# Eleven row groups of w2 by column halves instead of thirteen, and another grouping of the output rows

## The chip, the cores and the metric

The kernel runs on one core of a Trainium2 chip. The metric is the device time of one execution in microseconds (us); lower is better. A core has a matrix engine (TensorE, "PE" in the profile, with its weight loads as "PEld"), a vector engine (VectorE, "DVE"), a scalar engine (ScalarE, "ACT"), GpSimd ("POOL") and SyncE ("SP"). In this kernel GpSimd hands over the loads and SyncE the stores. The data are moved by 16 DMA engines that all queues share. Matmul results land in PSUM, in eight banks of 128 partitions x 512 f32, and have to be evicted from there to SBUF by VectorE or ScalarE before they can be stored.

## What is computed

Attention with eightfold mean-pooled keys and values (8 batches, 8 heads, 576 positions, 64 per head) gives 4608 tokens x of width 512. A soft mixture of experts follows, with 8 experts of 4 slots each (32 slots). The change touches only what stands in the last lines, the second layer and the combine.

```
logits = x @ phi                               # 4608 x 32
d = softmax of logits over the tokens;  slot_input = d.T @ x
for e in range(8):
    h = max(slot_input[e] @ w1[e], 0)          # 4 x 1024
    slot_out[e] = h @ w2[e]                    # w2[e]: 1024 x 512
c = softmax of logits over the slots
out = c @ slot_out                             # 4608 x 512, f32
```

All weights come as f32 and are turned into bf16 by the loads.

## The kernel before, in words

Until about 112 us the kernel runs the attention in four pairs of batches. The weights w1 and w2 stream in behind the attention's inputs, all through GpSimd's one queue, in the order in which the code issues them.

**w2 and its pieces.** The 1024 rows of one expert's w2 lie in SBUF as 128 partitions x 8 row groups (`FJ` = 8) of 512 columns. Experts 0 to 3 go to `big` and 4 and 5 to `qTa`, whole. Expert 6 (`E - 2`) is cut: its first `CUT6` = 3 row groups come in full width (line 507). Its other five, and all eight of expert 7 (`E - 1`), come by column halves of 256 columns, `halves` (line 91): first all thirteen groups for the left half, then all thirteen for the right. `PIECES` (line 92) lists them: five groups of expert 6, then four, three and one of expert 7, one DMA each (lines 526 to 533). So the left half of `slot_out` is complete before the right half of the last weights has arrived, and the left half of the output can be stored meanwhile. `half_home` gives each piece its place in `xsa`.

**The second layer.** `second_layer` (line 576) adds row groups into the one PSUM tile `so_ps`. TensorE's order is written out by hand (lines 680 to 711). Between the pieces stand dummy matmuls, `busy(n)` (line 611), which write to a tile nobody reads, so that TensorE isn't idle.

**The tail.** `begin(half, stores)` (line 652) ends one column half. For the first four tiles of 128 tokens (`CARRY` = 4) the last row group isn't waited for twice: ScalarE copies what `so_ps` holds without it, scaled, to `so_a`, and four matmuls on `zT` (line 659) put the last group's share straight into the output banks; four more (line 662) add the rest from `so_a`. Then the last row group goes into `so_ps` (line 663), VectorE copies it to `so` (line 667), and from `so` come all other tiles (`product`, line 636). Each tile is evicted with the scale of its rows by `put(n, cols, engine, ps)`, where engine 0 is ScalarE (line 616) and 1 VectorE (line 618). `tiles(n0, n1, half)` does two tiles and stores them. Tiles 0 to 9 are done by halves, left then right; the other 26 in full width after that. Five PSUM banks turn over for these products.

**The grouping of the rows.** `GROUPS` (line 57) says how many rows of the output each partition holds in a group of tiles: 2, 2, 2, 4, 4, 8 and 14, 36 tiles in all. Tile r of a group of n rows holds the tokens base + n x p + r for partition p, so that a group of n rows is stored with n rows of 512 f32 in one run per partition. `tokens(n)` (line 456) picks the right columns of `cT`. `out_a` (the space of `exa`) holds the first six tiles on their way out, `out_b` (the space of `w1_sb`) the others (lines 623 to 630).

**The stores.** SyncE issues them in the order of the code: for the left half four stores of one tile each (in `begin`) and three of two tiles; for the right half five of two tiles; then a group of 4, one of 8 and one of 14 rows in full width, 1, 2 and 3.5 MB.

Of the kernel before, what the change touches and what calls it, by code (L numbers as in the profile page):

```python
# [18 lines left out]
def kernel(  # L19
# [10 lines left out]
    nc = tc.nc  # L30
# [5 lines left out]
    E = moe_w1.shape[0]  # L36
# [12 lines left out]
    FJ = F // 128  # L49
# [4 lines left out]


    GROUPS, base = [], 0
    for rows in (2, 2, 2, 4, 4, 8, 14):
        GROUPS.append((rows, base))
        base += 128 * rows
    TILES = [(g, r) for g, (rows, _) in enumerate(GROUPS) for r in range(rows)]  # L60
# [13 lines left out]
    cT = persist.tile([128, 2, B * S // 2], BF)  # L74
# [11 lines left out]

    CUT6 = FJ - 5
    HC = DM // 2  # L90
    halves = [slice(0, HC), slice(HC, DM)]
    PIECES = ((E - 2, CUT6, FJ), (E - 1, 0, 4), (E - 1, 4, FJ - 1), (E - 1, FJ - 1, FJ))

# [15 lines left out]
    def load_w2(home, e, n, j0=0, j1=FJ):  # L109
        for i in range(n):  # L110
            for j in range(j0, j1):
                w2_at[e + i, j] = home[:, i, j * DM:(j + 1) * DM]
        nc.gpsimd.dma_start(out=home[:, 0:n, j0 * DM:j1 * DM],
                            in_=moe_w2[e:e + n].rearrange("e (p j) d -> p e j d", j=FJ)[:, :, j0:j1].rearrange("p e j d -> p e (j d)"))
# [49 lines left out]
    with tc.tile_pool(name="tmp", bufs=1) as tmp:  # L164
# [8 lines left out]
        for r in range(2):  # L173
            rows = slice(r * D, (r + 1) * D)
# [11 lines left out]
        for r in range(2):  # L186
            rows = slice(r * D, (r + 1) * D)
# [219 lines left out]
    for g, (rows, base) in enumerate(GROUPS):  # L407
        cols = cT[:, :, base // 2:base // 2 + 64 * rows].rearrange("p r (i s) -> p s r i", s=rows // 2)
# [44 lines left out]
        nc.vector.reciprocal(out=recR[:, 2:4, 0:len(quads)], in_=ps[:, 2:4, 0:len(quads)])  # L453
        yield

    def tokens(n):

        g, r = TILES[n]
        rows, base = GROUPS[g]
        step, c0 = rows // 2, base // 2 + r // 2  # L460
        return cT[:, r % 2, c0:c0 + 127 * step + 1:step]

    def step(gen):
        if gen is not None:
# [41 lines left out]
    load_w2(qTa, 4, 2)  # L506
    load_w2(xsa[:, 0:1], E - 2, 1, 0, CUT6)

# [8 lines left out]
    def half_home(e, half):  # L517
        if e == E - 1:
            flat = xsa[:, 1, half * FJ * HC:(half + 1) * FJ * HC]
        else:  # L520
            c0 = CUT6 * DM + half * (FJ - CUT6) * HC
            flat = xsa[:, 0, c0:c0 + (FJ - CUT6) * HC]
        return flat.rearrange("p (j c) -> p j c", c=HC)

    w2_half = {}
    for half, cols in enumerate(halves):
        for e, j0, j1 in PIECES:
            home = half_home(e, half)
            i = 0 if e == E - 1 else CUT6
            nc.gpsimd.dma_start(out=home[:, j0 - i:j1 - i],  # L530
# [17 lines left out]
    recC = post.tile([128, 1], FP)  # L548
# [25 lines left out]
    so_ps = ps_o.tile([128, DM], FP, name="so_ps")  # L574

    def second_layer(e, j0=0, j1=FJ, half=None, by=1):

        cols = slice(0, DM) if half is None else halves[half]
        for fj in range(j0, j1):
            g = fj % NG  # L580
            rhs = w2_at[e, fj] if half is None else w2_half[e, fj, half]
            nc.tensor.matmul(out=so_ps[g * NS:(g + 1) * NS, cols].rearrange("p (c s) -> p s c", s=by), lhsT=hT[:, e, fj],  # L582
                             rhs=rhs.rearrange("p (c s) -> p s c", s=by),
                             start=(e == 0 and fj < NG), stop=(e == E - 1 and fj >= NG), skip_group_check=True)
# [12 lines left out]
    J7 = FJ - 1  # L597
# [3 lines left out]
    CARRY = 4  # L601
    z_ps = ps_f.tile([128, 2, 128 * CARRY // 2], FP, name="z_ps", tag="f")
    nc.tensor.matmul(out=z_ps, lhsT=hz, rhs=cT[:, :, 0:128 * CARRY // 2], start=True, stop=True)
    zT = post.tile([128, 2, 128 * CARRY // 2], BF)
# [6 lines left out]
    def busy(n):  # L611
        nc.tensor.matmul(out=idle[:, 0:n], lhsT=cTf[:, 0:128], rhs=cTf[:, 0:n], start=True, stop=True)

    def scaled(engine, dst, src, by):
        if engine == 0:
            nc.scalar.activation(out=dst, in_=src, func=AF.Copy, scale=by)  # L616
        else:
            nc.vector.tensor_scalar(out=dst, in0=src, scalar1=by, scalar2=None, op0=ALU.mult)  # L618

    so_a = post.tile([128, DM], BF)  # L620
    so = post.tile([128, DM], BF)

    out_a = exf.rearrange("p (n c) -> p n c", c=DM)
    out_b = w1f.rearrange("p (n c) -> p n c", c=DM)
    n = 0
    places = []
    for rows, base in GROUPS:
        home = out_a[:, n:n + rows] if n + rows <= 6 else out_b[:, n - 6:n - 6 + rows]
        places.append((home, out[base:base + 128 * rows].rearrange("(p r) c -> p r c", r=rows)))
        n += rows  # L630

    def store(g, r0, r1, cols):
        home, dst = places[g]
        nc.sync.dma_start(out=dst[:, r0:r1, cols], in_=home[:, r0:r1, cols])

    def product(n, cols):
        bank = ps_f.tile([128, DM], FP, name="f_ps", tag="f")
        rhs, times = so[:, cols], 2 if cols == halves[0] and n >= CARRY else 1
        nc.tensor.matmul(out=bank[:, 0:times * (cols.stop - cols.start)].rearrange("p (a c) -> p a c", a=times), lhsT=tokens(n),  # L639
                         rhs=rhs.rearrange("p c -> p () c").to_broadcast([128, times, cols.stop - cols.start]),  # L640
                         start=True, stop=True)
        return bank[:, 0:cols.stop - cols.start]

    def rec(n):
        i, c = place[n]
        return recR[:, i, c:c + 1]

    def put(n, cols, engine, ps):
        g, r = TILES[n]
        scaled(engine, places[g][0][:, r, cols], ps, rec(n))  # L650

    def begin(half, stores):

        cols = halves[half]
        scaled(0, so_a[:, cols], so_ps[:, cols], recC)
        f = []
        for n in range(CARRY):
            f.append(ps_f.tile([128, DM], FP, name="f_ps", tag="f")[:, 0:HC])
            nc.tensor.matmul(out=f[n], lhsT=zT[:, n % 2, n // 2 * 128:n // 2 * 128 + 128], rhs=w2_half[E - 1, J7, half],
                             start=True, stop=False)  # L660
        for n in range(CARRY):
            nc.tensor.matmul(out=f[n], lhsT=tokens(n), rhs=so_a[:, cols], start=False, stop=True)
        second_layer(E - 1, J7, FJ, half)
        put(0, cols, 0, f[0])
        put(1, cols, 1, f[1])
        put(2, cols, 0, f[2])
        scaled(1, so[:, cols], so_ps[:, cols], recC)
        put(3, cols, 0, f[3])
        for g, r0, r1 in stores:
            store(g, r0, r1, cols)  # L670

    def tiles(n0, n1, half):

        cols = halves[half]
        for n in range(n0, n1):
            put(n, cols, 1 - n % 2, product(n, cols))
        g, r = TILES[n0]
        store(g, r, r + n1 - n0, cols)

# [7 lines left out]
    busy(512)  # L687
    second_layer(E - 2, 0, CUT6)
    busy(512)
# [3 lines left out]
    second_layer(*PIECES[1], 0)  # L693
    busy(192)
    second_layer(*PIECES[2], 0)
    begin(0, ((0, 0, 1), (0, 1, 2), (1, 0, 1), (1, 1, 2)))
    for n in (4, 6):
        tiles(n, n + 2, 0)
    for e, j0, j1 in PIECES[:2]:
        second_layer(e, j0, j1, 1)  # L700
    tiles(8, 10, 0)
    for e, j0, j1 in PIECES[2:-1]:
        second_layer(e, j0, j1, 1)
    begin(1, ((0, 0, 2), (1, 0, 2)))
    for n in (4, 6, 8):
        tiles(n, n + 2, 1)
    for n in range(10, len(TILES)):
        g, r = TILES[n]
# [33 lines left out]
```

## Time and profile before

| | us |
|---|---|
| median of 3 runs | 174.50 (174.48 to 174.53) |
| the profiled execution | 174.42 |
| its span, from the first to the last instruction | 172.6 |
| TensorE busy | 131.7 (76%) |
| VectorE busy | 100.8 (58%) |
| ScalarE busy | 88.0 (51%) |
| load queue, share of the 16 DMA engines | 87.0% |
| store queue (and one early load), share of the 16 DMA engines | 15.5% |

The span is what the trace shows; the profiled execution's own time has 1.8 us more around it. A row of the timeline reads: start, duration, engine, line, operation, what it writes and reads, how often, and in brackets how long the engine stood idle before it and what ended that. "L616" is line 616 of the kernel; several instructions in a row that are alike are merged into one row. In the rows of stages the columns are the stretch, its length, the busy time and number of instructions of each engine, then the clock that TensorE was granted, the busy share of the DMA engines (packets that overlap on one engine are added, so it can exceed 1) and the rate in GB/s. A row of the DMA list ends with the size of one transfer and the time from its issue to its landing.

### The profile page before, as it was taken

Reading aid. Unit: us, or ns where it says so; the run is one execution under the profiler, and the core shown is the slowest. Engines: PE = TensorE matmul, PEld = TensorE weight load, DVE = VectorE, ACT = ScalarE, POOL = GpSimd, SP = SyncE. Lnnn points to the kernel's source line nnn. Section 1 sums busy time; section 2 is a strip of 40 time slices with the busy share of each in tenths; the row PEclk is TensorE's granted clock in tenths of the full one; section 3 lists DMA queues with packets and bytes.
Section 4 is the critical chain, followed back from the end, with each engine's and each line's share of the span. In section 5 each row is a group of like instructions: output and inputs, shape, how many; then the busy total and the mean of one; then the engine's idle time right before and its main releaser. Section 6 shows DMA issues by size and latency. Waiting matters only on the chain.

```text
span 172.6 us, 2869 instructions
## 1 busy us (share of the span) xinstructions
PE 131.7 (76%) x1106; PEld 71.1 (41%) x1106; DVE 100.8 (58%) x265; ACT 88.0 (51%) x168; POOL 27.5 (16%) x42
## 2 busy tenths in 40 slices
PE   0005798899999999899789999896899997899000
PEld 0002373556555656556345554452452234433000
DVE  6686152569678667887994858841551103599300
ACT  3201336988496846988601998566021003699100
POOL 7000102020201013205100470130610030000000
PEclk9999999999999999999999999999999999999955
DMA  5999999999999999999999999999999999999994
GB/s 196 244 220 222 209 220 218 209 219 218 209 218 217 216 219 214 216 217 211 218 216 215 216 216 220 216 213 216 216 215 216 208 193 195 321 354 425 490 425 213
DMA packets 10589, 41.13 MB, mean 238 GB/s; under 512 B 704, under 2 KB 6592, under 8 KB 6864
## 3 DMA queue, kind: packets, MB, share of 16 engines
q0 software_dynamic: 7248, 30.48, 87.0%
q1 hardware_dynamic: 3328, 10.49, 15.5%
q8 instruction: 8, 0.13, 0.3%
q14 instruction: 5, 0.04, 0.1%
HBM read 61.93 MB, written 9.44 MB: 413 GB/s over the span
## 4 chain that ended last, share of the span: by engine, by line
PE 34%; DMA 27%; ACT 14%; DVE 13%; issue 3%; POOL 1%; DVEq 0%; ACTq 0%; POOLq 0%
DMA xsa<-in_moe_w_dram 21%; PE pool_ps L232 10%; ACT exa L311 7%; DMA phi_f<-in_moe_phi_dram 7%; DVE xsa L342 6%; PE u_ps L331 5%; PE q_ps L264 5%; PE sc L309 5%; PE G_ps L366 3%; PE turn_ps L248 2%; DVE w_sb L618 2%; ACT vmeans L238 2%; PE f_ps L639 2%; ACT vp L296 2%; ACT w_sb L616 1%
## 5 line engine op out<-in xcount | busy, mean ns | idle before, releaser
L311 ACT ACTIVATE exa<-sc 72x576 bf16<-72x576 f32 x64 | 39.3, 653 | 4.6 <-PE sc L309 3.8
L342 DVE TENSOR_TENSOR xsa<-u_ps,rec 128x384 bf16<-128x384 f32 x69 | 37.8, 554 | 1.7
L331 PE MATMUL u_ps<-vp,exa 128*128 128x97 bf16 (+5 forms) x320 | 31.4, 229 | 3.6 <-DVE xsa L342 3.0
L331 PEld LDWEIGHTS <-exa 128*128 128x128 bf16 (+1 forms) x320 | 18.9, 100 | 15.7 <-DVE xsa L342 6.4
L309 PE MATMUL sc<-qTa,kp 64*72 64x288 bf16 x128 | 20.6, 303 | 1.7 <-ACT exa L311 1.2
L232 PE MATMUL pool_ps<-big,pmat 128*128 128x512 bf16 x64 | 18.2, 410 | 0.7 <-ACT qTa L268 0.7
L336 DVE RECIPROCAL rec<-u_ps 128x4 f32<-128x4 f32 x72 | 11.9, 174 | 10.8 <-PE u_ps L331 10.5
L268 ACT COPY qTa<-q_ps 128x768 bf16<-128x768 bf16 x8 | 6.4, 794 | 13.1 <-PE q_ps L264 13.1
L184 PE MATMUL phi_ps<-spread,sel 128*128 128x256 bf16 x4 | 1.3, 395 | 15.0 <-DVE spread L179 15.0
L264 PE MATMUL q_ps<-ident,big 128*128 128x128 bf16 x144 | 12.4, 230 | 0.2
L639 PE MATMUL f_ps<-so,cT 128*128 128x512 bf16 (+1 forms) x38 | 10.1, 361 | 2.0 <-DVE so L618 1.3
L240 DVE TENSOR_REDUCE rsum<-rest_ps 128x64 f32<-128x512 f32 x8 | 5.5, 691 | 10.1 <-PE rest_ps L236 10.1
L309 PEld LDWEIGHTS <-kp 64*72 64x72 bf16 x128 | 7.8, 107 | 8.9 <-issue 3.5
L618 DVE TENSOR_SCALAR w_sb<-f_ps,recR 128x512 f32<-128x512 f32 (+1 forms) x17 | 10.5, 679 | 0.6 <-PE f_ps L639 0.5
L264 PEld LDWEIGHTS <-big 128*128 128x128 bf16 x144 | 9.6, 103 | 2.5 <-issue 1.0
L270 DVE COPY qTa<-q_ps 128x768 bf16<-128x768 bf16 x16 | 8.7, 551 | 2.6 <-PE q_ps L264 2.6
L616 ACT ACTIVATE w_sb<-f_ps,recR 128x512 f32<-128x512 f32 (+1 forms) x17 | 9.5, 637 | 0.7 <-PE f_ps L639 0.5
L530 POOL DMA_DIRECT2D xsa<-in_moe_w_dram x8 | 5.9, 743 | 22.3 <-DMA qTa<-in_moe_w_dram 8.9
L366 PE MATMUL G_ps<-xsa,ee 128*128 128x512 bf16 x36 | 8.4, 379 | 1.2 <-ACT ee L361 1.2
L232 PEld LDWEIGHTS <-pmat 128*128 128x128 bf16 x64 | 6.0, 102 | 6.9 <-issue 2.4
L238 ACT CAST vmeans<-pool_ps 128x1024 bf16<-128x1024 f32 x4 | 4.0, 1012 | 6.8 <-PE pool_ps L232 6.8
L616 ACT ACTIVATE so_a<-so_ps,recC 128x256 bf16<-128x256 f32 x2 | 0.9, 470 | 12.4 <-PE so_ps L582 12.4
(109 smaller groups left out, 168.8 us busy)
## 6 DMA issues: line engine op xcount, KB each, us to landing
w_sb<-in_moe_w_dram POOLq DMA_DIRECT2D x2, 3072.0 KB, 36.7
big<-in_q_dram POOLq DMA_DIRECT2D x4, 1152.0 KB, 12.5
big<-in_v_dram POOLq DMA_DIRECT2D x4, 1152.0 KB, 15.8
big<-in_moe_w_dram POOLq DMA_DIRECT2D x1, 4096.0 KB, 33.3
out_dram<-w_sb SPq DMA_DIRECT2D x1, 3584.0 KB, 10.6
big<-in_k_dram POOLq DMA_DIRECT2D x3, 1152.0 KB, 21.3
w_sb<-in_moe_w_dram POOLq DMA_DIRECT2D x2, 1024.0 KB, 18.3
qTa<-in_moe_w_dram POOLq DMA_DIRECT2D x1, 2048.0 KB, 30.1
```

What stands on the lines that cost most here:

```text
L232: nc.tensor.matmul(out=ps, lhsT=pmat, rhs=src[:, t:full * POOL:POOL, :], start=(t == 0), stop=(t == POOL - 1))
L264: nc.tensor.transpose(out=ps[:, t].rearrange("p n i -> p (n i)"), in_=q_sb[pair][:, tt:tt + 2, :].rearrange("p t d -> p (t d)"), identity= ...
L270: nc.vector.tensor_copy(out=dst, in_=ps)
L309: nc.tensor.matmul(out=ps[:, r, 0:S // 2], lhsT=kp[pair][rows, n], rhs=qT[pair][rows, n].rearrange("p t i -> p (t i)"), start=True, stop=True)
L311: nc.scalar.activation(out=dst.rearrange("p r (i t) -> p r i t", t=NU), in_=ps[:, :, 0:S // 2].rearrange("p r (t i) -> p r i t", i=NI), fu ...
L331: nc.tensor.matmul(out=bank[rows, hh * UW:(hh + times) * UW].rearrange("p (a c) -> p a c", a=times), lhsT=ex[b][:, hh].rearrange("p r t -> ...
L336: nc.vector.reciprocal(out=rec, in_=ps[:, :, XW])
L342: nc.vector.tensor_tensor(out=dst, in0=ps[:, :, 0:XW], in1=rec.rearrange("p h -> p h ()").to_broadcast([128, HQ, XW]), op=ALU.mult)
L366: nc.tensor.matmul(out=ps, lhsT=ee[:, t].rearrange("p g s -> p (g s)"), rhs=x[:, t, :, 0:D], start=(t == 0), stop=(t == 8))
L616: nc.scalar.activation(out=dst, in_=src, func=AF.Copy, scale=by)
L618: nc.vector.tensor_scalar(out=dst, in0=src, scalar1=by, scalar2=None, op0=ALU.mult)
L639: nc.tensor.matmul(out=bank[:, 0:times * (cols.stop - cols.start)].rearrange("p (a c) -> p a c", a=times), lhsT=tokens(n), rhs=rhs.rearran ...
```

## The change

Three things change, all in the tail. `CUT6` goes from 3 to 5, so that expert 6 has five row groups in the full-width piece and three by column halves; eleven groups are left in halves. The output's groups become 4, 6, 4, 8 and 14 rows: the first four tiles are one group, the next six another. In the left half's `begin` the last row group is added to `so_ps` after the first of the four matmuls on `so_a` instead of after the fourth, VectorE copies `so` before it evicts anything, and tile 1 goes to ScalarE and tile 3 to VectorE; the left half's tiles 4 to 9 swap engines. The stores of the first four tiles are one, one and two tiles in the left half (four single ones before), and one, two and one in the right half (two of two tiles before). The number of stores stays fifteen.

```
-    for rows in (2, 2, 2, 4, 4, 8, 14):
+    for rows in (4, 6, 4, 8, 14):
...
-    CUT6 = FJ - 5
+    CUT6 = FJ - 3
...
+    def of_tile(t, n):
         g, r = TILES[n]
         rows, base = GROUPS[g]
         step, c0 = rows // 2, base // 2 + r // 2
-        return cT[:, r % 2, c0:c0 + 127 * step + 1:step]
+        return t[:, r % 2, c0:c0 + 127 * step + 1:step]
+    def tokens(n):
+        return of_tile(cT, n)
...
-        home = out_a[:, n:n + rows] if n + rows <= 6 else out_b[:, n - 6:n - 6 + rows]
+        home = out_a[:, n:n + rows] if n + rows <= 4 else out_b[:, n - 4:n - 4 + rows]
...
-            nc.tensor.matmul(out=f[n], lhsT=zT[:, n % 2, n // 2 * 128:n // 2 * 128 + 128], rhs=w2_half[E - 1, J7, half],
+            nc.tensor.matmul(out=f[n], lhsT=of_tile(zT, n), rhs=w2_half[E - 1, J7, half],
                              start=True, stop=False)
         for n in range(CARRY):
             nc.tensor.matmul(out=f[n], lhsT=tokens(n), rhs=so_a[:, cols], start=False, stop=True)
-        second_layer(E - 1, J7, FJ, half)
+            if n == (0 if half == 0 else CARRY - 1):
+                second_layer(E - 1, J7, FJ, half)
         put(0, cols, 0, f[0])
-        put(1, cols, 1, f[1])
-        put(2, cols, 0, f[2])
-        scaled(1, so[:, cols], so_ps[:, cols], recC)
-        put(3, cols, 0, f[3])
-        for g, r0, r1 in stores:
-            store(g, r0, r1, cols)
+        if half == 0:
+            scaled(1, so[:, cols], so_ps[:, cols], recC)
+            put(1, cols, 0, f[1])
+            put(2, cols, 0, f[2])
+            put(3, cols, 1, f[3])
+        else:
+            put(1, cols, 1, f[1])
+            put(2, cols, 0, f[2])
+            scaled(1, so[:, cols], so_ps[:, cols], recC)
+            put(3, cols, 0, f[3])
+        for r0, r1 in stores:
+            store(0, r0, r1, cols)
...
-            put(n, cols, 1 - n % 2, product(n, cols))
+            put(n, cols, (n + half) % 2, product(n, cols))
...
-    begin(0, ((0, 0, 1), (0, 1, 2), (1, 0, 1), (1, 1, 2)))
+    begin(0, ((0, 1), (1, 2), (2, 4)))
...
-    begin(1, ((0, 0, 2), (1, 0, 2)))
+    begin(1, ((0, 1), (1, 3), (3, 4)))
```

More of the change, by code (lines that the diff above doesn't have):

```diff
@@ L454, in slot_sums @@
         yield
-    def tokens(n):
+    def of_tile(t, n):
         g, r = TILES[n]
```

## The prediction

> **What bounds the kernel now.** I began with the page's slices. The DMA line holds at full from the second slice to the last but one, so the question is not which compute engine is busiest but whether the DMA engines ever wait, and for what.
>
> ```profile
> DMA  5999999999999999999999999999999999999994
> ```
>
> The chain of waits names the two loads that end the load phase: the full-width piece of the sixth of eight experts' weights counted from zero (the one the change enlarges) lands at 112.32 + 27.64 = 139.96, and the last piece of all, one row group of the second column half, lands at 148.69.
>
> ```profile
> 112.32 27.64 DMA xsa<-in_moe_w_dram
> ...
> 140.51 8.18 DMA xsa<-in_moe_w_dram
> 148.69 0.05 issue
> ```
>
> Then I asked for stages, with the DMA rate in the last column (loads count what is written, half of what is read, since they turn f32 into bf16).
>
> ```profile
> 130.00:138.00 8.00, 8.00 (x43) 2.21 (x41) 1.01 (x2) 0.59 (x1) 0.00 (x0) 1.00 1.02 212
> 144.00:146.50 2.50, 1.78 (x13) 1.15 (x13) 0.96 (x2) 1.68 (x4) 0.00 (x0) 1.00 1.45 196
> 148.50:149.00 0.50, 0.43 (x6) 0.24 (x4) 0.13 (x1) 0.50 (x2) 0.00 (x0) 1.00 0.87 301
> 149.00:151.00 2.00, 1.35 (x12) 0.90 (x10) 0.97 (x2) 1.41 (x4) 0.00 (x0) 1.00 1.06 365
> 151.00:151.50 0.50, 0.42 (x4) 0.22 (x3) 0.48 (x2) 0.37 (x1) 0.00 (x0) 1.00 0.73 248
> 151.50:152.00 0.50, 0.44 (x2) 0.19 (x2) 0.50 (x3) 0.50 (x3) 0.00 (x0) 1.00 1.02 342
> 152.00:155.00 3.00, 2.80 (x12) 1.18 (x11) 2.85 (x5) 3.00 (x6) 0.00 (x0) 1.00 1.04 347
> 155.00:162.50 7.50, 4.51 (x16) 1.76 (x14) 6.08 (x10) 5.07 (x9) 0.00 (x0) 1.00 1.04 432
> 162.50:171.40 8.90, 0.00 (x0) 0.00 (x0) 0.00 (x0) 0.00 (x0) 0.00 (x0) 0.59 0.96 412
> ```
>
> Three things are to be seen. Full-width loads run at 212 GB/s, column-half loads at 196. Stores of half rows (1 KB runs) run near 350 to 365, whole-row stores near 432. And the drain has only two soft spots: 148.5 to 149.0, at 301 instead of 365, (1 - 301/365) x 0.5 = 0.09 us lost, and 151.0 to 151.5, at 248, 0.16 us lost. So the end is: loads, then 9.44 MB of stores, with a quarter of a microsecond of holes. Nothing that the change does shrinks the stores: the same twenty half tiles, 2.6 MB, go in 1 KB runs, and the last three stores (1, 2 and 3.5 MB) are untouched.
>
> SyncE's queue shows when the stores are handed over.
>
> ```profile
> 145.68 2.52 SPq L634 DMA_DIRECT2D out_dram<-exa  x5
> 148.32 1.07 SPq L634 DMA_DIRECT2D out_dram<-w_sb  x2
> 150.23 1.93 SPq L634 DMA_DIRECT2D out_dram<-exa  x3
> 152.27 9.22 SPq L634 DMA_DIRECT2D out_dram<-w_sb  x5
> ```
>
> The first seven are the first column half, handed over by 149.39. The second half's first comes at 150.23, and the hole at 151.0 ends around 151.4, so a store needs about 1.1 to 1.2 us from its issue to its first bytes (an estimate from these two rows). That is the hole's cause: the first half's stores run out before the second half's arrive.
>
> **The change, part by part.**
>
> *Loads.* Two row groups of that expert move from column halves (4 x 64 KB) into the full-width piece (256 KB, 0.262 MB). Gone: 0.262 / 0.196 = 1.34 us. Added: 0.262 / 0.212 = 1.24 us. That is a gain of 0.10. The other bound comes from when the matmuls that wait for the pieces start:
>
> ```profile
> 140.24 0.40 PE L582 MATMUL so_ps<-xsa,hT 128*32 128x512 bf16 x3
> 140.57 1.12 PE L612 MATMUL idle_ps<-cT 128*128 128x512 f32 x2
> 141.73 0.38 PE L582 MATMUL so_ps<-xsa,hT 128*32 128x256 bf16 x5
> 142.04 0.41 PE L451 MATMUL RT_ps<-identf,sums 10*128 10x10 f32 x4
> 142.38 0.59 PE L612 MATMUL idle_ps<-cT 128*128 128x192 f32 x2
> 143.05 0.29 PE L582 MATMUL so_ps<-xsa,hT 128*32 128x256 bf16 x4
> 143.27 0.59 PE L612 MATMUL idle_ps<-cT 128*128 128x192 f32 x2
> 144.02 0.29 PE L582 MATMUL so_ps<-xsa,hT 128*32 128x256 bf16 x3 [0.15 <-DMA xsa<-in_moe_w_dram]
> 144.37 0.60 PE L659 MATMUL f_ps<-xsa,zT 128*128 128x256 bf16 x4
> 144.88 0.60 PE L662 MATMUL f_ps<-so_a,cT 128*128 128x256 bf16 x4
> 145.40 0.28 PE L582 MATMUL so_ps<-xsa,hT 128*32 128x256 bf16 x1
> 146.33 0.38 PE L639 MATMUL f_ps<-so,cT 128*128 128x512 bf16 x1 [0.65 <-DVE so L618]
> ```
>
> The five-group piece comes 141.69 - 139.96 = 1.73 us after the full one (141.73 less the 0.04 us hand-over that the chain shows elsewhere, 148.69 to 148.74); the three-group piece behind it takes 144.02 - 143.05 = 0.97. Making five into three thus saves 0.76 per half, 1.52 for both, against the 1.24 added: a gain of 0.28. Ends 0.10 and 0.28; I take 0.2, the middle, since one is a mean of all 16 DMA engines and the other the slowest of them, and both count. In time: the full piece lands at 139.96 + 1.24 = 141.20, the first half's pieces all come 1.24 - 0.76 = 0.48 later than now (0.57 by the rates), and the last landing moves from 148.69 to about 148.5.
>
> The Trainium skill, "DMA: Bandwidth & Descriptors", section "Specifications", gives 512 B as the least transfer for line rate; the column-half pieces write just 512 B a run, so by it the moved row groups would gain nothing. This trace disagrees, 196 against 212.
>
> *GpSimd's queue.* The last load waits there for the full piece (139.96, issued 140.51, landed 8.18 later). Now it is issued about 141.75. Between the full piece and that last load stand 21 half groups of 64 KB, 7 us at 196 GB/s, so the later issue is covered with over 5 us. Cost nothing; without that cover it would be 1.24.
>
> *TensorE's fillers.* The dummy matmuls stand between the pieces in a fixed order, and the pieces after the full one now come closer to it. Full piece 141.25: five matmuls of 512 columns (0.33 for three now, a fifth adds one more pass, 0.21) to 141.8; the 512-column filler (140.57 to the next landing, under 1.16; the earlier ones follow at 1.05) to 142.85, while the three-group piece was there at 142.2; its matmuls 0.22, the transposes 0.34, the filler of 192 about 0.55, to 143.95; four matmuls 0.22 and a filler 0.55, to 144.75, while that piece landed near 144.5. So TensorE is late by about 0.25, and the first half starts 0.48 + 0.25 = 0.73 later than now, not 0.48.
>
> *Order within the first half.* Four evictions and the copy `so` are dealt anew.
>
> ```profile
> 144.35 0.47 ACT L616 ACTIVATE so_a<-so_ps,recC 128x256 bf16<-128x256 f32 x1 [12.39 <-PE so_ps L582]
> 145.18 1.20 ACT L616 ACTIVATE exa<-f_ps,recR 128x256 f32<-128x256 f32 x3 [0.36 <-PE f_ps L662]
> ```
>
> ```profile
> 145.80 0.48 DVE L618 TENSOR_SCALAR so<-so_ps,recC 128x256 bf16<-128x256 f32 x1
> ```
>
> Now `so` waits for the last of four matmuls, then for a fifth, then stands behind an eviction on VectorE. After the change that fifth comes second, and `so` is VectorE's first: with a pitch of (0.60 - 0.28) / 3 = 0.11 in that group of four, it starts at about 145.40 - 3 x 0.11 = 145.07 on today's times, and `so` about 0.45 sooner against its own inputs. Shifted by 0.73: `so_a` at 145.08, tile 0 evicted by 146.38 and its store issued near 146.4 (today 145.68), `so` at 146.1, the first product at 146.6 (today 146.33), so the first half's last evictions end near 148.75 (ScalarE's, tile 8). The first store is 0.7 late, the first half's end only 0.2 to 0.3 late at most. Of the first four tiles ScalarE keeps three and VectorE one, and tiles 4 to 9 are dealt three and three as now, so neither engine gets more work; only the order changes.
>
> *What the late first store costs.* It reaches the DMA engines at 146.4 + 1.1 = 147.5 rather than 146.8. The loads end engine by engine; the slowest has work until about 148.4 in either kernel. The early ones will idle, up to 0.7 us, the average over 16 perhaps 0.3. But these same engines idle at 151 today because they are ahead of the slowest, which is never starved. I bound it 0 to 0.3 and take 0.05, nearest to the slowest engine, which ends last.
>
> *The hole at 151.* The first half's stores now end later against the last landing, and the second half's first store waits for one eviction, not two (single row, then two, then one). Its issue moves from 150.23 to about 149.9. The hole should shrink: gain 0 to 0.16, I take 0.05, as most of it falls to engines that are ahead anyway.
>
> *What stays.* Count of stores (15; from the ninth of SyncE's transfers on each waits for the one eight before it, which landed long ago by the queue's rows, and that shift by one costs nothing), evictions of the second half, products, and the grouped sums (ten rows before and after). Strided weights for the first tiles replace contiguous ones; later tiles already have them. Cost nothing, hidden by the evictions.
>
> *Limit of the gain.* A DMA that is ahead needs its next store.
>
> ```profile
> 156.55 0.34 SPq L634 DMA_DIRECT2D out_dram<-w_sb  x1
> ...
> 161.16 0.33 SPq L634 DMA_DIRECT2D out_dram<-w_sb  x1
> ```
>
> The 2 MB store is at the engines at 156.55 + 1.1 = 157.65; it lands at 156.55 + 6.7 = 163.25, and 2.1 MB at 432 take 4.9, so it begins near 158.0 with the landing's lag. The slack is 0.3. The second half's evictions, which set that issue, move earlier by 0.1 to 0.2 with the last landing. So more than about 0.45 cannot come.
>
> ```profile
> out_dram<-w_sb SPq DMA_DIRECT2D x1, 3584.0 KB, 10.6
> ...
> out_dram<-w_sb SPq DMA_DIRECT2D x1, 2048.0 KB, 6.7
> ```
>
> Sum: -0.20 (loads) + 0.05 (late start) - 0.05 (hole) = -0.20. The profiled execution took 174.42 us around its 172.6 span; 174.42 - 0.20 = 174.22. The median of the runs is 174.50, 0.08 above, so I say 174.3 for the median.
>
> **Rivals.**
>
> *Both holes close and the loads give all* (faster). -0.28 - 0.09 - 0.16 = -0.53, cut by the 2 MB store's slack to about -0.45: 174.05. For it: the first half's last stores and the second half's first move towards each other. Against: the slowest engine has no hole to lose.
>
> *The backlog on TensorE carries through* (slower). Place: ScalarE at the start of the second half. If the first half's slip of 0.73 is not caught up by the earlier `so`, the last first-half eviction ends at about 149.5, `so_a` of the second half stands behind it rather than behind the last landing, and every later issue, the 2 MB store's too, slips 0.7. Less its slack of 0.3, the DMA engines wait 0.4: 174.9. It decides from the point where ScalarE's eviction of tile 8 starts after about 148.3, the time that the last landing asks for `so_a` less one eviction pitch. For it: ScalarE is only just free there today. Against: its last eviction of the half is now tile 8's, not tile 9's, and `so` is early.
>
> *Nothing happens*: the column-half loads cost no more than full ones, and the holes merely move: 174.5. By the Trainium skill's rule above it would be this. Against it stand the two rates.
>
> **How the numbers follow.** Forecast 0.42, faster rival 0.28, slower rival 0.22, nothing 0.08. 0.2% is 0.35 us, about what a measurement of this kernel can tell from no change. The forecast lies within it but for its edges, which I give 0.04 to faster and 0.02 to slower; nothing lies within. Faster 0.32, same 0.42 + 0.08 - 0.06 = 0.44, slower 0.24. The range: 173.9 (the faster rival and a little) to 174.95 (the slower rival); the forecast's own is 174.1 to 174.6.
>
> **What would show it.** Right: the full piece lands near 141.2, the last load near 148.5, first store issued near 146.4, the second half's first near 149.9, the 151 hole mostly gone, the 3.5 MB store's issue 0.1 to 0.3 before 161.16, landing about 0.2 before 171.8. Wrong: the last landing not before 148.65 (load term), a hole over 0.5 us wide in the mean at 147 (late start), or ScalarE's second `so_a` after 148.9 (the backlog).

## The result, and the profile after

| | before | after |
|---|---|---|
| median of the runs (range), us | 174.49 (174.41 to 174.75) | 174.80 (174.61 to 175.38) |
| profiled execution, us | 174.42 | 174.67 |
| its span, us | 172.6 | 172.9 |
| last load landed, us | 148.69 | 148.56 |
| first store issued / last store landed, us | 145.68 / 171.72 | 146.26 / 171.96 |

The ratio after to before is 1.0018, interval 1.0012 to 1.0024: 0.3 us slower. That lies within the 0.2% that the prediction called no change, and inside its range, but it has the other sign than the forecast of 174.3.

The page's DMA line for the kernel after is as full as before, so the slices alone don't show the loss.

```profile
DMA  5999999999999999999999999999999999999994
```

The chain of waits of the kernel after (start, duration, what) answers to the load steps.

```profile
111.81 29.34 DMA xsa<-in_moe_w_dram
141.15 0.04 issue
141.19 0.59 PE so_ps L585 x5
141.78 1.05 PE idle_ps L615 x2
...
144.15 0.52 PE idle_ps L615 x2
144.67 0.22 PE so_ps L585 x3
144.88 0.02 issue
...
146.05 0.49 DVE so L621
146.54 0.04 issue
146.59 1.02 PE f_ps L642 x4
```

The full piece lands at 141.15 (forecast 141.20), `so` runs at 146.05 (146.1) and the first product at 146.59 (146.6). These three times were foreseen to a tenth of a microsecond. ScalarE's second `so_a`, in the same kernel's timeline of that engine, stands where it stood before (148.74):

```profile
148.75 0.47 ACT L619 ACTIVATE so_a<-so_ps,recC 128x256 bf16<-128x256 f32 x1
```

SyncE's queue after:

```profile
146.26 1.75 SPq L637 DMA_DIRECT2D out_dram<-exa  x3
148.12 1.55 SPq L637 DMA_DIRECT2D out_dram<-w_sb  x3
150.08 1.60 SPq L637 DMA_DIRECT2D out_dram<-exa  x3
151.79 9.72 SPq L637 DMA_DIRECT2D out_dram<-w_sb  x6
```

The first store is 0.58 later than before (forecast 0.7), and the second half's first comes at 150.08 (from 150.23; forecast 149.9). What this does is in the windows after (last column GB/s).

```profile
148.00:148.50 0.50, 0.50 (x5) 0.09 (x3) 0.13 (x1) 0.19 (x1) 0.00 (x0) 1.00 0.67 208
148.50:149.00 0.50, 0.50 (x7) 0.34 (x8) 0.48 (x1) 0.50 (x2) 0.00 (x0) 1.00 1.01 338
149.00:151.00 2.00, 1.32 (x11) 0.82 (x9) 0.98 (x3) 1.43 (x4) 0.00 (x0) 1.00 1.04 346
151.00:151.50 0.50, 0.44 (x5) 0.26 (x3) 0.46 (x2) 0.35 (x1) 0.00 (x0) 1.00 1.03 342
152.00:155.00 3.00, 2.80 (x12) 1.15 (x11) 2.85 (x5) 3.00 (x6) 0.00 (x0) 1.00 1.04 342
```

Before, the first of these windows read:

```profile
148.00:148.50 0.50, 0.45 (x5) 0.19 (x3) 0.35 (x1) 0.13 (x1) 0.00 (x0) 1.00 1.06 333
```

So the hole at 151 did close, 342 for 248, but another opened at 148, 208 for 333, and between them the half-row stores ran at 346 instead of 365. The hole at 148 goes with a slow hand-over. In SyncE's queue the third store, of two tiles, took 0.84 us to hand over; everything behind it waited. Which of the two brings the other the trace doesn't say.

```profile
147.18 0.84 SPq L637 DMA_DIRECT2D out_dram<-exa  x1
```

The clearest ledger is what had been stored at a given time: the store queue's row in the list of DMA queues (packets, MB, share), first up to 149, then up to 155. Before:

```profile
q1 hardware_dynamic: 498, 0.46, 14.9%
...
q1 hardware_dynamic: 2643, 2.53, 49.7%
```

After:

```profile
q1 hardware_dynamic: 416, 0.39, 13.0%
...
q1 hardware_dynamic: 2571, 2.45, 49.3%
```

By 149, 0.07 MB is missing. From 149 to 151 the lower rate takes (365 - 346) x 2.0 = 0.04 MB, the closed hole at 151 gives 0.05 back, 152 to 155 takes 0.015. That is the 0.08 MB missing at 155. Both kernels are still storing half rows then, at 342 to 347 GB/s, so the whole rows start 0.08 / 0.345 = 0.23 us later (an estimate), and the last landing is 0.24 late. The loads gave 0.13; the stores had lost more before the second half began.

### The profile page after: what moved, and what is told of

Read it like the earlier page. It is cut to its first block, busy times and chain, and to the rows that moved or that the text cites. A ratio compares the mean times of both kernels' runs of the same rounds, so it can differ in the third digit from the quotient of the medians.

```text
span 172.9 us, 2864 instructions
## 1 busy us (share of the span) xinstructions
PE 130.7 (76%) x1104; PEld 69.7 (40%) x1104; DVE 100.6 (58%) x265; ACT 88.2 (51%) x168; POOL 27.3 (16%) x42
## 4 chain that ended last, share of the span: by engine, by line
PE 37%; DMA 24%; DVE 16%; ACT 12%; issue 3%; POOL 1%; DVEq 0%; ACTq 0%; POOLq 0%
DMA xsa<-in_moe_w_dram 17%; PE pool_ps L232 10%; ACT exa L311 7%; DMA phi_f<-in_moe_phi_dram 7%; DVE xsa L342 6%; PE u_ps L331 5%; PE sc L309 5%; PE q_ps L264 4%; DVE w_sb L621 4%; PE G_ps L366 3%; PE f_ps L642 2%; PE turn_ps L248 2%; ACT vmeans L238 2%; DVE rsum L240 2%; ACT vp L296 2%
## 5 line engine op out<-in xcount | busy, mean ns | idle before, releaser
L264 PE MATMUL q_ps<-ident,big 128*128 128x128 bf16 x144 | 11.6, 219 | 0.8 <-DVE qTa L270 0.3
L621 DVE TENSOR_SCALAR w_sb<-f_ps,recR 128x512 f32<-128x512 f32 (+1 forms) x19 | 11.3, 661 | 1.2 <-PE f_ps L642 0.7
L619 ACT ACTIVATE w_sb<-f_ps,recR 128x512 f32<-128x512 f32 (+1 forms) x19 | 10.3, 622 | 1.0 <-DMA xsa<-in_moe_w_dram 0.4
L264 PEld LDWEIGHTS <-big 128*128 128x128 bf16 x144 | 8.7, 97 | 3.0 <-issue 1.4
```

The source lines that it names most:

```text
L264: nc.tensor.transpose(out=ps[:, t].rearrange("p n i -> p (n i)"), in_=q_sb[pair][:, tt:tt + 2, :].rearrange("p t d -> p (t d)"), identity= ...
```

## Experiments

Each difference is to the kernel before unless another is named; "time" is the median of the timed runs. Every kernel computes the whole result. The thirteen and eleven are the numbers of row groups that are loaded by column halves.

**Eleven groups alone.**

```
-    CUT6 = FJ - 5
+    CUT6 = FJ - 3
```

> The kernel before with only the eleven groups (CUT6 = FJ - 3); rows, stores and evictions as before. Late-start theory (the left half begins about 0.6 us later, the DMA engines whose loads end first find no store): first store issued near 146.3 instead of 145.68, last load landing near 148.55, a hole before 148.6 as in the changed kernel, and, since the copy so is not moved forward here, a second hole near 151; 0.3 to 0.6 us slower than before. Layout theory (groups of 4 and 6 rows make the half-row stores slower, 346 instead of 365 GB/s between 149 and 151): the rows are the old ones, so the last load's gain of 0.13 us stands alone and it is 0.1 us faster.

Measured: 175.02, ratio 1.0026 (1.0015 to 1.0037), +0.52. The first store goes at 146.32 and the last load lands at 148.62. With `so` in its old place, and so late as well, there is a hole in 149 to 151 (281 GB/s for 365):

```profile
149.00:151.00 2.00, 1.44 (x12) 0.88 (x10) 0.94 (x3) 1.64 (x5) 0.00 (x0) 1.00 0.84 281
```

So the part that was to bring the gain costs half a microsecond by itself.

**New rows and stores alone**, thirteen groups, old order; `of_tile` and the split between `out_a` and `out_b` are as in the change.

```
-    for rows in (2, 2, 2, 4, 4, 8, 14):
+    for rows in (4, 6, 4, 8, 14):
...
-    begin(0, ((0, 0, 1), (0, 1, 2), (1, 0, 1), (1, 1, 2)))
+    begin(0, ((0, 1), (1, 2), (2, 4)))
...
-    begin(1, ((0, 0, 2), (1, 0, 2)))
+    begin(1, ((0, 1), (1, 3), (3, 4)))
```

> The kernel before with only the new grouping (4, 6, 4, 8, 14 rows) and its stores; thirteen groups and the evictions as before. Late-start theory: the first store is issued near 145.7 as before, no hole before 148.4, the time within 0.1 us of before. Layout theory: the half-row stores run near 346 GB/s instead of 365 right from 149, and it is 0.25 to 0.4 us slower.

Measured: 174.17, ratio 0.9982 (0.9973 to 0.999), -0.33. This, which I had priced at nothing, is the only part that helps. The second half's store of tiles 6 and 7 is handed over faster in this kernel, where they belong to a group of six rows,

```profile
152.19 0.44 SPq L637 DMA_DIRECT2D out_dram<-w_sb  x1
```

than before, where they belong to a group of four:

```profile
152.27 0.56 SPq L634 DMA_DIRECT2D out_dram<-w_sb  x1
```

**New left order alone.**

```
-        second_layer(E - 1, J7, FJ, half)
+            if n == (0 if half == 0 else CARRY - 1):
+                second_layer(E - 1, J7, FJ, half)
...
+        if half == 0:
+            scaled(1, so[:, cols], so_ps[:, cols], recC)
+            put(1, cols, 0, f[1])
...
-            put(n, cols, 1 - n % 2, product(n, cols))
+            put(n, cols, (n + half) % 2, product(n, cols))
```

> The kernel before with only the left half's new order: the last row group after the first matmul on so_a, the copy so first on VectorE, tiles 1 and 3 and 4 to 9 on the other engine. Thirteen groups, old rows, old stores. Late-start theory: the first store as before (145.7), the later left stores up to 0.3 us earlier, the soft spot at 148.5 to 149 filled and the one at 151 unchanged or longer by as much; 0 to 0.15 us faster than before. Layout theory: the same. If it is slower by over 0.15 us, the order itself costs something that neither names.

Measured: 174.51, ratio 0.9999 (0.999 to 1.0008). No difference that can be seen.

**The change with thirteen groups.**

```
-    CUT6 = FJ - 3
+    CUT6 = FJ - 5
```

> The changed kernel with thirteen groups again (CUT6 = FJ - 5), new rows, stores and evictions. Late-start theory: the first store is back at 145.7, no hole before 148.4, and it is level with before or up to 0.15 us faster, so 0.3 us or more faster than the changed kernel. Layout theory: it keeps the slower stores and stays 0.25 to 0.4 us slower than before.

Measured: 174.16, ratio 0.9981 (0.9972 to 0.9989), -0.34. First store 145.75, last load 148.76. It beats both kernels, and against it the eleven groups of the change land the last load 0.20 sooner (0.13 in the repeat of the change further down, at 148.63), and yet end 0.64 later by these medians.

**The first store late.** From the kernel with thirteen groups, the first half's first three stores go as one, which waits for all four tiles.

```
-    begin(0, ((0, 1), (1, 2), (2, 4)))
+    begin(0, ((0, 4),))
```

> Thirteen groups with the new rows and order (0.34 us faster than before), but the left half's first three stores are made one of four tiles: the loads and all evictions stay, only the first store is issued about 0.9 us later (near 146.7 instead of 145.75). My prediction's view (the DMA engines that finish their loads early are ahead anyway, the slowest one ends last and is never starved): level with the thirteen-group kernel, within 0.1 us. Shared-throughput theory (bytes not stored while early engines idle are lost for good, whoever is ahead): about 0.08 to 0.12 MB less stored by 149, at 0.35 MB per us 0.2 to 0.35 us slower than the thirteen-group kernel.

Measured: 174.78, ratio to before 1.0012 (1.0 to 1.0024); against the thirteen-group kernel +0.62 by medians, 0.54 by the two ratios. Its SyncE queue begins:

```profile
146.59 0.61 SPq L637 DMA_DIRECT2D out_dram<-exa  x1
147.31 2.43 SPq L637 DMA_DIRECT2D out_dram<-w_sb  x3
```

The stored bytes of this kernel by 149 and by 155,

```profile
q1 hardware_dynamic: 356, 0.36, 11.9%
...
q1 hardware_dynamic: 2518, 2.43, 48.7%
```

and of the thirteen-group kernel:

```profile
q1 hardware_dynamic: 533, 0.51, 16.5%
...
q1 hardware_dynamic: 2739, 2.68, 52.0%
```

0.15 MB is lost directly by 149. The figure by 155 overstates what goes afterwards: just before 155 the thirteen-group kernel already begins to store whole rows, in packets of 8 KB that are counted in full when they begin. Up to 154 only half rows are stored, and the same row of the list reads 2.09 MB for the late store and 2.28 MB for the thirteen-group kernel. At 0.35 MB per us, the rate of the half-row stores, 0.15 MB are 0.43 us, and the 0.19 MB by 154 are 0.54. The windows show both parts. Late first store:

```profile
147.00:148.00 1.00, 0.93 (x12) 0.34 (x11) 0.66 (x2) 0.44 (x2) 0.00 (x0) 1.00 1.01 159
149.20:150.40 1.20, 0.97 (x8) 0.58 (x6) 0.61 (x2) 0.84 (x4) 0.00 (x0) 1.00 1.04 342
```

Thirteen groups:

```profile
147.00:148.00 1.00, 0.94 (x12) 0.34 (x11) 0.61 (x2) 0.39 (x1) 0.00 (x0) 1.00 1.29 259
149.20:150.40 1.20, 0.92 (x8) 0.53 (x6) 0.65 (x2) 0.84 (x4) 0.00 (x0) 1.00 1.07 371
```

The same half-row stores move at 342 instead of 371 after the late start; by 154 that has cost no more than the further 0.04 MB. Two stores fewer is also part of this edit, and the three stores behind the first take 0.55 to 0.94 us to hand over instead of 0.37 to 0.45.

**Is it TensorE's backlog?** The kernel after, with the filler ahead of expert 6's left-half piece cut.

```
-    busy(512)
+    busy(192)
```

> The changed kernel (eleven groups) with the filler ahead of expert 6's left-half piece cut from 512 to 192 columns. TensorE was 0.06 to 0.13 us late at the left half's last three-group piece there; without it the first store is issued about 0.1 us earlier. Backlog theory (the slip on TensorE is the cause): at least 0.2 us faster than the changed kernel. Late-landing theory (the load's order, not TensorE, sets the start): 0 to 0.1 us faster.

**The kernel after, once more**, on the chip of the kernel without fillers below.

> The changed kernel itself, beside the kernel without fillers on one chip. If the shorter filler's 0.19 us was a difference between chips, this has 174.6 here; if the filler did it, 174.75 to 174.85.

Measured: 174.61 with the short filler and 174.63 unchanged, on two chips, each beside the kernel before (ratios 1.0001, 0.9992 to 1.0011, and 1.0008, 1.0 to 1.0017). The first store goes at 146.27 with the filler cut, at 146.26 and 146.33 in the two runs with it whole. With the filler cut, TensorE waits for the landing of expert 7's left three-group piece, and starts on it when the kernel after does (first the short filler, then the kernel after):

```profile
144.60 0.29 PE L585 MATMUL so_ps<-xsa,hT 128*32 128x256 bf16 x3 [0.17 <-DMA xsa<-in_moe_w_dram]
```

```profile
144.60 0.29 PE L585 MATMUL so_ps<-xsa,hT 128*32 128x256 bf16 x3
```

So the landing of the pieces sets the start to within 0.1 us, not TensorE, and the backlog falls as a cause. The short-filler kernel shows the slow third hand-over and the hole again (0.93 us; 219 GB/s in 148.0 to 148.5). The repeat's profiled run took another course than the first one. Its third store was handed over in half the time,

```profile
147.24 0.41 SPq L637 DMA_DIRECT2D out_dram<-exa  x1
```

its windows show neither the hole nor the lower rate,

```profile
148.00:148.50 0.50, 0.50 (x8) 0.09 (x5) 0.20 (x1) 0.13 (x1) 0.00 (x0) 1.00 0.98 323
...
149.20:150.40 1.20, 0.92 (x7) 0.49 (x5) 0.62 (x2) 0.84 (x4) 0.00 (x0) 1.00 1.07 365
```

and it took 174.51. By 149 it had stored 0.46 MB, as much as the kernel before, and by 154 2.22 MB, where the kernel before had 2.17 and thirteen groups had 2.28. So the hole at 148 is not needed for the loss against thirteen groups; it may be why the change's runs spread up to 175.38. Against the kernel before, this run was not behind in bytes at all, and its last store still landed 0.08 later, at 171.80: a landing is recorded in sixteen steps, which I take for the sixteen DMA engines, and those of the last store lie 0.42 us apart here, 0.18 in the kernel before. The last engine sets the end.

**Old rows, the new lists as far as they allow**, from the kernel before.

```
-    begin(0, ((0, 0, 1), (0, 1, 2), (1, 0, 1), (1, 1, 2)))
+    begin(0, ((0, 0, 1), (0, 1, 2), (1, 0, 2)))
...
-    begin(1, ((0, 0, 2), (1, 0, 2)))
+    begin(1, ((0, 0, 1), (0, 1, 2), (1, 0, 2)))
```

> The kernel before, with the old rows of 2, 2, 2, 4, and only the list of stores of the first four tiles changed: one, one, two tiles in the left half, one, one, two in the right (fifteen in all). If the gain of 0.33 us of the new grouping comes from when stores are handed over, this has most of it, 0.2 to 0.35 us faster than before; if it comes from where the rows lie in memory, it is within 0.1 us of before.

**New rows, the other list for the second half**, from the thirteen-group kernel.

```
-    begin(1, ((0, 1), (1, 3), (3, 4)))
+    begin(1, ((0, 1), (1, 2), (2, 4)))
```

> The thirteen-group kernel with the new rows, but the right half's first four tiles stored one, one, two instead of one, two, one. If the gain of 0.33 us of the new grouping is the list (one, two, one puts three tiles instead of two before the second half's wait), this loses it: a hole near 152 as with the old rows and this list, 174.45 or more. If it is the rows (stores of two tiles handed over in 0.37 to 0.45 us instead of 0.53 to 0.56), it keeps most: 174.3 or less.

**Six-row group alone**, from the kernel before, with `out_a` for four tiles as in the change.

```
-    for rows in (2, 2, 2, 4, 4, 8, 14):
+    for rows in (2, 2, 6, 4, 8, 14):
```

> The kernel before with groups of 2, 2, 6, 4, 8 and 14 rows: tiles 4 to 9 become one group as in the change, tiles 0 to 3 keep two rows a partition, all stores and evictions as before. Rows theory: the right half's stores of tiles 4 to 9 are handed over in 0.37 to 0.45 us, 0.1 to 0.25 us faster than before. List theory: within 0.08 us of before.

Measured: old rows with new lists 174.52, ratio 0.9996 (0.9987 to 1.0004); new rows with the other list 174.20, 0.9986 (0.9978 to 0.9995); six-row group alone 174.61, 1.0007 (0.9998 to 1.0015). The gain needs the new rows; the lists alone bring none, and neither does the six-row group without the four-row one ahead of it. New rows with the old lists were not tried. With the old rows the hole moves rather than goes. Old rows, new lists, three windows:

```profile
149.20:150.40 1.20, 0.93 (x8) 0.58 (x6) 0.64 (x2) 0.83 (x4) 0.00 (x0) 1.00 1.06 367
...
152.00:152.50 0.50, 0.50 (x3) 0.20 (x2) 0.35 (x2) 0.50 (x3) 0.00 (x0) 1.00 0.61 209
...
152.60:154.80 2.20, 2.00 (x9) 0.74 (x8) 2.20 (x4) 2.20 (x5) 0.00 (x0) 1.00 1.04 345
```

Six-row group alone:

```profile
151.00:151.50 0.50, 0.46 (x5) 0.28 (x3) 0.44 (x2) 0.33 (x1) 0.00 (x0) 1.00 0.48 168
```

In the first of them a single kernel goes from 367 to 345 with a hole between, on stores of the same run length. The repeat of the change goes from 365 to 344 in the first and last of these windows without one.

**How many groups by halves?** The kernel with new rows and fifteen, fourteen and twelve.

```
-    CUT6 = FJ - 5
+    CUT6 = FJ - 7      (fifteen; FJ - 6 fourteen, FJ - 4 twelve)
```

> The thirteen-group kernel with new rows and order, but fifteen groups by column halves (CUT6 = FJ - 7): the left half starts about 0.55 us earlier still, the loads end 0.1 to 0.25 us later. Shared-throughput theory: with thirteen the engines that finish early hardly idle before 148.5, so an earlier start buys nothing there, the loads' loss remains and the hole near 151 grows; 0.1 to 0.4 us slower than thirteen. If every 0.5 us of earlier start were worth what it is from eleven to thirteen (0.64 us), it would be 0.4 us or more faster.

> New rows, stores and order with fourteen groups (CUT6 = FJ - 6), between thirteen (174.16) and fifteen (174.28). Starvation-and-step theory: no hole at 148 in either, so only the loads' price of half width, about 0.06 us a group: 174.2 to 174.25, rate and skew like thirteen's. If there is an optimum it is thirteen or fourteen, within 0.1 us of each other.

> New rows, stores and order with twelve groups by column halves (CUT6 = FJ - 4), between thirteen (174.16) and eleven (174.80). Starvation-and-step theory (a hole at 148 costs its idle time once, and then the engines run their half-row stores in step and about 7% slower): the first store is issued near 146.0; if a hole opens at 148, the rate between 149.2 and 150.4 drops to about 335 packets per us from 360 and the time is near that of eleven, 174.5 or more; if none opens, the skew between the DMA engines stays over 0.5 us and it is within 0.15 us of thirteen. Linear theory (each 0.25 us of later start costs its share): 174.45 to 174.5 with the rate halfway.

| groups by halves | time, us | ratio to before | first store | last load |
|---|---|---|---|---|
| 15 | 174.28 | 0.9986 (0.9978 to 0.9995) | 145.25 | 148.88 |
| 14 | 174.22 | 0.9983 (0.9975 to 0.9992) | 145.66 | 148.91 |
| 13 | 174.16 | 0.9981 (0.9972 to 0.9989) | 145.75 | 148.76 |
| 12 | 174.28 | 0.9985 (0.9976 to 0.9993) | 145.95 | 148.64 |
| 11 (the change; time of the repeat, profile of the first) | 174.63 | 1.0008 (1.0 to 1.0017) | 146.26 | 148.56 |

Twelve to fifteen can't be told apart; eleven falls off. Twelve's runs lie evenly between 173.97 and 174.44, and the profiled one, 174.01, is among the fastest. It kept the high rate,

```profile
149.20:150.40 1.20, 0.80 (x6) 0.47 (x5) 0.78 (x2) 0.91 (x3) 0.00 (x0) 1.00 1.07 370
```

and had 2.32 MB stored by 154, the most of all.

**No fillers.** The kernel after without the three dummy groups between the first half's pieces.

```
-    busy(512)
...
-    busy(192)
...
-    busy(192)
```

> The changed kernel without the three fillers that stand between the pieces of the left half (512, 192, 192 columns). Backlog theory: TensorE is never late at a piece, the first store comes up to 0.1 us earlier and it is 0.2 us or more faster than the changed kernel beside it. Late-landing theory: the landings set the start, 0 to 0.1 us faster. If TensorE's granted clock falls before 160 us, the tail is slower by more than that and the run says nothing about the backlog.

Measured: 175.57, ratio 1.0062 (1.0047 to 1.0077). It was meant to free TensorE; it took its clock away instead (the column ahead of the last two is the granted clock).

```profile
143.00:145.00 2.00, 0.64 (x8) 0.35 (x8) 0.38 (x2) 0.07 (x1) 0.00 (x0) 1.00 1.45 194
145.00:147.00 2.00, 2.00 (x10) 0.97 (x10) 0.52 (x2) 1.35 (x4) 0.00 (x0) 0.58 1.41 190
147.00:149.00 2.00, 2.00 (x12) 0.47 (x11) 1.21 (x3) 1.32 (x4) 0.00 (x0) 0.57 1.04 266
```

It says nothing on the backlog, then, but gives the fillers' worth: 0.94 us against the unchanged kernel beside it.

**Four single stores in the first half**, from the kernel after.

```
-    begin(0, ((0, 1), (1, 2), (2, 4)))
+    begin(0, ((0, 1), (1, 2), (2, 3), (3, 4)))
```

> The changed kernel with its left half's first four tiles stored one by one (four stores, sixteen in all). In the slower of two traces of the changed kernel SyncE spent 0.84 us on handing over the third, two-tile store, and the hole at 148 followed; in the faster trace 0.41 us. If that hand-over makes the hole, single tiles reach the DMA engines sooner: no hole over 0.1 us at 148, 174.4 to 174.6. If the late first store alone makes it, the hole stays and it is 174.6 to 174.8 as the changed kernel.

Measured: 175.37, ratio 1.0048 (1.0036 to 1.006). The hole at 148 is gone (326 GB/s), and still it is slower; the half-row stores run at 338 in 149.2 to 150.4. Its last store lands at 172.06, 0.10 after the change's, but its span goes on to 173.4 and its profiled run took 175.17; in the change only 0.94 stands behind the last landing, here 1.34. I have no explanation for that tail, so nothing is built on its time.

## Why the prediction was right and wrong, step by step

The whole splits into new rows -0.33, new order 0, and eleven groups for thirteen +0.47 to +0.64 (174.63 or 174.80 against 174.16), which gives the +0.14 to +0.31 measured for all.

*Loads, -0.20: right in sign, and 0.13 in size.* 148.69 to 148.56. With everything else equal it is 148.76 to 148.56, or to 148.63 in the repeat. In the thirteen-group kernel and in the repeat the full piece had landed 0.05 to 0.06 later than in the kernels before and after (140.02 for 139.96, 141.20 for 141.15), so these two are the like pair, and they give 0.13 again. It lies nearer to the 0.10 from the rates than to the 0.28 from the waits. The Trainium skill's 512 B rule, by which the moved groups would gain nothing ("DMA: Bandwidth & Descriptors", section "Specifications"), is not borne out here.

*GpSimd's queue covered, and the timing of the first half: right.* The first store came at 146.26, not 146.4, since TensorE was late by about 0.05 rather than 0.25 (the matmuls on expert 7's left three groups start 3.41 us after those on the full piece, 3.36 with the short filler).

*"What the late first store costs": the step that failed.* I wrote "I bound it 0 to 0.3 and take 0.05, nearest to the slowest engine, which ends last". The late-store kernel puts 0.54 to 0.62 on 0.84 us of lateness, with the loads where they were: 0.15 MB not stored by 149 (0.43 us) and 0.04 MB more by 154. My mean idle time over all engines, 0.3, was nearer to the first part than the 0.05; wrong was to discount it because the early engines "are ahead anyway", and to close the bound there. The bytes that the early engines don't store are not made up by being ahead. The MB stored by 154 follow the profiled times in order but for one pair:

```
stored by 154, MB   2.00   2.09   2.11   2.17   2.22   2.28   2.32
profiled run, us  174.93 174.92 174.67 174.42 174.51 174.13 174.01
(left to right: eleven alone, late store, after, before, after again, new rows with thirteen, with twelve)
```

0.32 MB go with 0.92 us, 0.35 MB per us, the rate of the half-row stores. Drawn through the kernel before, that line meets the other profiled runs within 0.1 us, but for three: the late store, the repeat of the change and the four single stores end 0.27, 0.23 and 0.6 later than it says. (The late store's profiled run is 0.14 above its median; in the repeat some 0.2 is the wide last landing.) So most of the differences are made before 154; that alone does not show why.

That lateness can make them is shown by the late-store kernel. How much of the change's loss it makes is open. Eleven groups for thirteen cost 0.47 to 0.64 although the loads gave 0.13, so 0.60 to 0.77 have to be found, and the first store is only 0.51 to 0.58 later. In proportion to the late-store kernel that is 0.33 to 0.43, an estimate. The rest differs between the two profiled runs: by 148, before the hole, the first had stored 0.12 MB where the kernel before had 0.15, by 148.5, with the hole, 0.22 for 0.31; the repeat lost no bytes by 149 against the kernel before, but its last engines ended late. That the half-row rate falls because of a hole is a correlation with exceptions: the repeat falls to 344 and the four single stores run at 338 without one, and the new order alone keeps 366 behind 262 at 148.5 to 149.

*The hole at 151, -0.05: the hole closed as forecast*, and its 0.05 MB came back, 0.14 us at the half-row rate. It also closes with new rows and stores alone (332 GB/s in 151.0 to 151.5), where nothing starts late, so the late start is not what closes it. The forecast did not see that a hole can open at 148 instead.

*"What stays", cost nothing: failed too*, in the other direction. The rows that group four and six tiles, with their stores, were worth -0.33. Whether by a shorter hand-over on SyncE or by where the rows lie in memory was not separated. The hand-over is not a property of the rows alone: two-tile stores take 0.44 to 0.62 in the kernel before, 0.37 to 0.46 with new rows and thirteen groups, but 0.41 to 0.84 with the same rows in the kernel after. The six-row kernel's right half takes 0.44 to 0.63, and it shows no gain.

*The rivals.* The backlog on TensorE did not carry through: `so_a` at 148.75 for the 148.9 that would have shown it, and a shorter filler changed nothing. The faster rival had both holes close, but did not ask whether a third would open. "Nothing" gave nearly the time, by luck: two terms of opposite sign nearly cancel, and it names neither.

## What to carry to other kernels

Where loads give way to stores on the same DMA engines, don't price a late first store by the slowest engine alone: 0.84 us of lateness cost 0.54 to 0.62 us here. Price it by the bytes not stored over all engines, at the rate of the stores that are held up (0.35 MB per us here), and look at the last landing too, since the last engine sets the end. When a change bundles several edits, price the ones "without cost" by an experiment as well: here the unpriced row grouping was the gain, and the edit it accompanied spent it. For this kernel, keep the new rows with thirteen groups, 174.16 us.

## What the runs showed of the hardware

- **Half-row stores have two rates.** In 149.2 to 150.4 the kernel after, the short filler, the late store and the four single stores moved 338 to 344 GB/s, and the others 359 to 375, the repeat among them, but for two with a hole inside that window (eleven groups alone, no fillers). The sixteen landing steps of the stores that land between 150.5 and 151.7 lie 0.27 to 0.50 us apart in the first kind, 0.65 to 1.8 in the second; so engines in step are the slower ones. Why was not tried.
- **One program, two courses.** The same store of the same kernel took 0.84 us to hand over in one profiled run and 0.41 in another, with a hole or none behind it.
- **The clock can fall without a long gap.** Without fillers TensorE's granted clock went to half from 145.31 to 148.72, 3.41 us, though no gap ahead of it was longer than 0.96 us; TensorE was busy 0.64 of the 2.00 us from 143 to 145, and 1.58 of the 3.41 us just ahead of the fall. The Trainium skill, "TensorE: Matmul & The Clock Gate", section "Part 1: The HAM clock gate (the "warmup" mystery)", gives a free-running window of about 3.4 us that halves the clock after an idle window. The length agrees; that whole windows without work are needed does not.
